# One more attention pair summed through a 128-column product, a weight difference made later, and a new block order at the start of the second product

## The chip, the cores and the metric

One core of a Trainium2 chip. The metric is device time in microseconds for one execution. Ratios are computed as the mean time of one kernel's fast runs over the mean of the other kernel's fast runs of the same rounds, so they are not quite the ratio of the medians that are quoted.

## The reference, cut to what matters

```
attention: batch 8, 8 heads, 576 positions, head size 64, window |i-j| <= 32
    attn = softmax(scale * q @ k.T inside the window);  a = attn @ v
x = a, heads side by side: 4608 x 512
h = x @ w_in (512 x 2048);  g = gelu_tanh(h);  out = g @ w_out (2048 x 512)
```

## The kernel before

The kernel walks over 9 tiles of 512 tokens. A tile first makes its hidden columns (`ffn_in`, then gelu on ScalarE), then the second product (`ffn_out`), into which the attention of the next batch is woven by a plan: at matmul number `i`, `s` makes scores, `m` multiplies by the mask, `v` makes the weighted sum, `x` normalises into `xT`. The digit is the pair (two of the eight heads, 0 to 3); 4 is the tail, the last positions of all pairs, and -1 the tail of the batch before. Tile 0 computes the second product plainly (`ffn_out_0`, 64 matmuls); later tiles use seven block products (112 matmuls) with sums of input blocks and four differences T1 to T4 of weight blocks. The differences are made once, by `combine`; T1 and T2 in tile 0, T3 and T4 in tile 1, where `i` is the number of the matmul ahead of which they are put on VectorE's queue.

```python
PLAN = {6: "s0 v-1", 24: "s1", 26: "m0", 31: "x-1", 40: "m1", 42: "v0 s2", 48: "x0", 56: "m2",
        61: "v1 s3", 64: "x1", 80: "m3", 81: "v2 s4", 88: "x2", 97: "v3", 104: "m4", 112: "x3"}
PLAN_0 = {0: "w0 w1 m0", 10: "s-1 m-1", ..., 51: "v3 c1 x3", 57: "s4 c2 m4"}    # w: cast weights, c: combine
ORDER_0 = ([(t4, 4 * w + i) for w in range(4) for t4 in (0, 1) for i in range(4)] + ...)
...
def cast_w(w, dst, on_dve=2, cs=range(4)):     # blocks 0, 1 on VectorE, 2, 3 on GpSimd
...
def weigh(b, g):                               # the weighted sum of pair g of batch b
    ...
        if fused(b, g):        # 8 products of 128 columns: V of one head beside ones
            ...
        else:                  # 16 products of 64 columns: V and ones, each for both heads
            ...
def invert(b, g, o, d):        # ScalarE: 1/sum as exp(-ln(sum)); fused: two logarithms of 64 rows
def spread(b, g, o, lt, d):    # VectorE: xT = sum * 1/sum; fused: two multiplications of 64 rows
...
todo={1: (T1, B12, B11), 2: (T2, B22, T1), 17: (T3, B22, B12), 33: (T4, B21, T2)}
```

Block product n = i // 16; product 5, so i = 80, is the first to read T4, which is B21 - T2. In the fused form one product of 128 columns gives the weighted sum of a head together with the sum by which it is divided; unfused, these are separate products of 64 columns. In VectorE's queue the changed kernel's T4 is written behind pair 1's normalisation.

The softmax here doesn't subtract the row's maximum and nothing guards it: scores larger than these inputs give would overflow.

Of the kernel before, what the change touches and what calls it, by code (L numbers as in the profile page):

```python
# [33 lines left out]
def width(pieces):  # L34
# [16 lines left out]
PLAN_0 = {0: "w0 w1 m0", 10: "s-1 m-1", 16: "s1 v-1 w2 m1 x-1", 24: "v0 s2 w3 x0", 32: "v1 m2 s3 x1",  # L51
          40: "v2 m3 x2", 48: "t4", 51: "v3 c1 x3", 57: "s4 c2 m4"}

ORDER_0 = ([(t4, 4 * w + i) for w in range(4) for t4 in (0, 1) for i in range(4)] +
           [(t4, fc) for t4 in (2, 3) for fc in range(16)])


FUSED = (3,)
# [6 lines left out]
def kernel(  # L65
# [9 lines left out]
    nc = tc.nc  # L75
# [4 lines left out]
    NF = DF // 128  # L80
# [8 lines left out]
    def load_table(which):  # L89
        nc.scalar.add_instruction(mybir.InstLoadActFuncSet(  # L90
            name=nc.get_next_instruction_name(), act_func_set_id=which, ins=[], outs=[]))
# [25 lines left out]
    Vs = [const.tile([128, 5, H + 1, 64], FP16, name=f"V{i}") for i in range(2)]  # L117
# [75 lines left out]
    def cast_w(w, dst, on_dve=2, cs=range(4)):  # L193
        for c in cs:
            (nc.vector if c < on_dve else nc.gpsimd).tensor_copy(dst[:, c, :], w[:, c, :])  # L195
# [37 lines left out]
    for i in (0, 3, 4, 1, 2):  # L233
        m, off = masks[i], 0
        for (k0, c, p0, p1) in kinds[i]:
# [6 lines left out]
                nc.vector.memset(m[k1:128, off:off + 4 * n], 0.0)  # L242
            off += 4 * n
    nc.vector.memset(ones, 1.0)
    nc.vector.memset(KTs[0][:, :, 576:640], 0.0)
    nc.vector.memset(Vs[0][64:128, 4, :, :], 0.0)

# [54 lines left out]
    def bank(i):  # L302

        return psM.tile([128, 512], FP32, name="mm", tag=f"x{i}")
# [76 lines left out]
    def fused(b, g):  # L381


        return b > 1 and g in FUSED

    def weigh(b, g, other=False):

# [68 lines left out]
    def ffn_in(t, n, d0=0, d1=4, then=True):  # L456
        fc = column(t, n)
        if n == 0 and d0 == 0:
            gTs[t] = gp.tile([128, NF, 512], FP16, name="gT", tag="gT")
        if d0 == 0:  # L460
            if t == 0 and 2 <= fc < 6:
                if fc % 2 == 0:
                    phs["S"] = psS.tile([128, 2, 512], FP32, name="ph2", tag=f"S{fc // 2 - 1}")
                phs[fc] = phs["S"][:, fc % 2, :]
            else:
                if t:
                    i = 3 if n in (1, 2) else 0 if n == 0 else (2, 1, 0)[n % 3]
                else:
                    i = fc if fc < 2 else (fc - 4) % 3
                if i == 3 and n == 1:  # L470
                    phs["S"] = psS.tile([128, 2, 512], FP32, name="ph3", tag="S0")
                phs[fc] = bank(i) if i < 2 else phs["S"][:, n - 1, :] if i == 3 else \
                    psO.tile([128, 512], FP32, name="ph", tag="D")
        ph = phs[fc]
        for dc in range(d0, d1):
            nc.tensor.matmul(ph, w_in16[:, dc, fc * 128:fc * 128 + 128],  # L476
                             xT[:, dc, t * 512 % RING:t * 512 % RING + 512],
                             start=(dc == 0), stop=(dc == 3))
        if d1 == 4 and then:
            gelu(t, n)  # L480

    def gelu(t, n):
        fc = column(t, n)
        nc.scalar.activation(gTs[t][:, fc, :], phs[fc], AF.Gelu_apprx_tanh)  # L484
        if t and n % 4 == 3:
            sums(t, n // 4)
# [3 lines left out]
    def combine_w():  # L490

        t12 = stage.tile([128, 2, 8, 256], FP16, name="t12", tag="stage")
        t34 = stage.tile([128, 2, 8, 256], FP16, name="t34", tag="stage")
        B11, B12, B21, B22 = (w_out16[:, r:r + 8, c:c + 256] for r in (0, 8) for c in (0, 256))
        T1, T2, T3, T4 = t12[:, 0], t12[:, 1], t34[:, 0], t34[:, 1]
        s12 = stage.tile([128, 2, 8, 256], FP16, name="s12", tag="stage")
        s34 = stage.tile([128, 2, 8, 256], FP16, name="s34", tag="stage")
        yo = stage.tile([128, 4, 512], FP32, name="y4", tag="stage")
        wino.update(B11=B11, B21=B21, B22=B22, T1=T1, T2=T2, T3=T3, T4=T4, S1=s12[:, 0],
                    S2=s12[:, 1], S3=s34[:, 0], S4=s34[:, 1], yo=yo,  # L500
                    todo={1: (T1, B12, B11), 2: (T2, B22, T1), 17: (T3, B22, B12),
                          33: (T4, B21, T2)})

    def combine(i):
        dst, x, y = wino["todo"][i]
        nc.vector.tensor_tensor(dst, x, y, op=ALU.subtract)  # L506
# [12 lines left out]
    pys = {}  # L519
# [3 lines left out]
    def store(t, t4, yo, cols=slice(0, 512), eng=None):  # L523
        m = 0
        while m < 128:
            b, c = divmod(t * 512 + t4 * 128 + m, S)
            q0, n = (0, cut(b)) if c < 4 * cut(b) else (cut(b), 144 - cut(b))
            j, p = divmod(c - 4 * q0, n)
            e = min(n - p, 128 - m)
            if t == NT - 1 and eng is None:  # L530
                turn_about.reverse()
            (eng or turn_about[0] if t == NT - 1 else eng or nc.gpsimd).dma_start(  # L532
                out_v[b, j, q0 + p:q0 + p + e, cols], yo[m:m + e, cols])
            m += e
# [1 line left out]
    later = []  # L536

    def ffn_out_0(t4, fc):
        if fc == 0:
            pys[t4] = bank(t4 % 2)  # L540
        nc.tensor.matmul(pys[t4], gTs[0][:, fc, t4 * 128:t4 * 128 + 128], w_out16[:, fc, :],  # L541
                         start=(fc == 0), stop=(fc == NF - 1))
        if fc == NF - 1:
            yo = yp.tile([128, 512], FP32, name="yo", tag="yo")
            nc.vector.tensor_copy(yo, pys[t4])
            if t4 == 3:
                store(0, t4, yo)
            else:
                later.append((t4, yo))
# [173 lines left out]
    for t in range(NT):  # L723
        b = t + 1
        att = b < B
        if t:
            for fc in range(begun):
                ffn_in(t, fc, 3, 4, then=False)
            for fc in range(begun):
                gelu(t, fc)  # L730
            if att and b > 1:
                cast_and_turn(b)
            for fc in range(begun, NF):
                ffn_in(t, fc)
        plan = PLAN_0 if not t else PLAN if att else {6: "v-1", 31: "x-1"} if t == B - 1 else {}

        def group(g):
            return (b, g) if g >= 0 else (b - 1, 4)

        if plan and t:  # L740
            load_table(exp_set)
        if t and b + 1 < B:
            load_qk(b + 1)
        ods = {}
        for i in range(113 if t else 65):
            for act in plan.get(i, "").split():
                kind, g = act[0], int(act[1:])
                if kind == "w":
                    cast_w(wo[g], w_out16[:, 4 * g:4 * g + 4, :])
                    if g == 2:  # L750
                        cast_v(1, 0)
                    if g == 3:
                        for pr in range(1, NPAIR):
                            cast_v(1, pr)
                        cast_vt(1)
                        cast_tails(1, nc.gpsimd)
                        load_qk(2)
                elif kind == "t":
                    pt = psS.tile([128, 2, 8, 128], FP16, name="pt", tag="S1")
                    trans_tails(1, pt[:, 0])  # L760
                elif kind == "c":
                    if g == 1:
                        combine_w()
                    combine(g)
                elif kind == "s":
                    score(*group(g))
                elif kind == "m":
                    mask(*group(g))
                elif kind == "v":
                    bb, gg = group(g)  # L770
                    o, d = weigh(bb, gg)
                    ods[g] = (o, *invert(bb, gg, o, d))
                    if t and g < 0 and b + 1 < B:
                        if t == 1:
                            nc.gpsimd.memset(Vs[1][:, :, 7, :], 1.0)
                        load_v(b + 1)
                    if t and g == (3 if att else -1):
                        load_table(gelu_set)
                else:
                    spread(*group(g), *ods[g])  # L780
            if t == 0 and i in (38, 40, 55):
                t4, yo = later.pop(0)
                store(0, t4, yo, eng=nc.scalar)
            if t == 0 and i < 64:
                ffn_out_0(*ORDER_0[i])
            elif t and i < 112:
                ffn_out(t, i)
        if t == 0:
            load_table(gelu_set)
            nc.gpsimd.memset(Vs[0][:, :, 7, :], 1.0)  # L790
            load_v(2)
        else:
            ffn_last(t)
        begun = 3 if att else 0
        for fc in range(begun):
            ffn_in(t + 1, fc, 0, 3)
# [28 lines left out]
```

## Time and profile before

| | before |
|---|---|
| median of 3 runs | 310.84 us (310.31 to 311.93) |
| span of the profiled run | 309.4 us |
| first matmul of tile 0's second product / tenth / seventeenth | 39.78 / 42.18 / 45.57 us |
| first matmul of tile 1 / of tile 2 | 60.67 / 92.89 us |
| TensorE's waits over 0.25 us from 39 us to tile 2 | 0.47 at the first, 0.36 at pair 1's sum in tile 1 |

A line of the timeline is start, duration, engine, source line, operation, out<-in, shapes and count, and in brackets the engine's idle time ahead of it and what ended it. A line of the waits view is who waited for whom, total us, times, longest. The lines themselves are in the prediction.

### The profile page before, as it was taken

What the parts mean: (1) busy time and instruction counts of PE and PEld (TensorE: products, weight loads), DVE (VectorE), ACT (ScalarE), POOL (GpSimd) and SP (SyncE); (2) the same over time, 40 slices, a digit from 0 to 9 for tenths busy, and PEclk for the clock granted to TensorE, in tenths of its full rate; (3) what the DMA queues carried; (4) which work ended last, traced back from release to release, by engine and by line L of the source; (5) the groups of instructions that cost most, each with busy time, mean ns of one, the idle gap of its engine ahead of it and who ended that gap; (6) DMA issues with size and microseconds to landing.
All of it is one profiled execution on the core that took longest, in us unless ns stands there. A gap on an engine that the chain in (4) does not pass through costs nothing.

```text
span 309.4 us, 6674 instructions
## 1 busy us (share of the span) xinstructions
PE 297.5 (96%) x2595; PEld 187.8 (61%) x2595; DVE 204.9 (66%) x461; ACT 201.9 (65%) x322; POOL 112.9 (36%) x173
## 2 busy tenths in 40 slices
PE   7889989999999999999999999999999999999993
PEld 3453545445784588448854775478647864784583
DVE  5764687787969677857786678766886654542451
ACT  1777476567677786778686877677768777606600
POOL 3658356096117420842075206720700070015000
PEclk9999999999999999999999999999999999999999
DMA  7999999999965999599859993999581031004013
GB/s 207 253 336 369 375 345 216 290 179 174 240 123 134 163 194 185 142 162 234 148 137 153 235 159 109 164 205 172 138 162 26 2 83 55 0 14 124 0 39 101
DMA packets 120254, 50.65 MB, mean 164 GB/s; under 512 B 101519, under 2 KB 113551, under 8 KB 120222
## 3 DMA queue, kind: packets, MB, share of 16 engines
q1 hardware_dynamic: 84329, 37.50, 53.6%
q0 software_dynamic: 34960, 11.54, 31.3%
q10 hardware_dynamic: 933, 1.18, 1.2%
q8 instruction: 20, 0.33, 0.4%
q14 instruction: 12, 0.10, 0.1%
HBM read 37.62 MB, written 9.44 MB: 152 GB/s over the span
## 4 chain that ended last, share of the span: by engine, by line
PE 82%; DMA 7%; SPq 5%; DVE 3%; issue 1%; POOL 1%; ACT 0%; POOLq 0%
PE mm L570 30%; PE mm L476 20%; PE ph L476 16%; PE ps_s L362 4%; PE mm L541 4%; PE ps_o L408 3%; DMA wst<-in_moe_w_out_dram 3%; DMA wst<-in_moe_w_in_dram 3%; PE ps_d L408 2%; SPq L134 2%; SPq L143 1%; POOL w_in L195 1%; SPq L186 1%; DVE t L506 1%; PE ps_o L399 1%
## 5 line engine op out<-in xcount | busy, mean ns | idle before, releaser
L476 PEld LDWEIGHTS <-w_in 128*128 128x128 f16 x576 | 56.1, 98 | 67.2 <-POOL w_in L195 1.6
L532 POOL DMA_DIRECT2D out_dram<-y x77 | 44.7, 588 | 114.8 <-DVE y L599 107.8
L476 PE MATMUL mm<-xT,w_in 128*128 128x512 f16 x320 | 78.2, 379 | 0.2 <-POOL w_in L195 0.2
L484 ACT ACTIVATE gT<-mm 128x512 f16<-128x512 f32 x80 | 47.6, 599 | 35.9 <-PE mm L476 35.2
L476 PE MATMUL ph<-xT,w_in 128*128 128x512 f16 x256 | 64.4, 379 | 0.9 <-ACT gT L484 0.7
L570 PEld LDWEIGHTS <-s 128*128 128x128 f16 x512 | 48.9, 98 | 7.0
L516 DVE TENSOR_TENSOR s<-gT 128x512 f16<-128x512 f16 x64 | 26.8, 419 | 34.4 <-ACT gT L484 34.4
L368 ACT ACTIVATE pe<-ps_s 128x704 f16<-128x704 f32 x64 | 43.3, 727 | 8.9 <-PE ps_s L362 8.0
L570 PE MATMUL mm<-t,s 128*128 128x256 f16 x376 | 45.8, 273 | 0.0
L484 ACT ACTIVATE gT<-ph 128x512 f16<-128x512 f32 x64 | 36.3, 602 | 12.3 <-PE ph L476 12.1
L570 PEld LDWEIGHTS <-gT 128*128 128x128 f16 x384 | 36.0, 98 | 7.3
L174 POOL DMA_DIRECT2D V<-in_v_dram x30 | 28.3, 964 | 23.0 <-PE ps_d L408 14.3
L426 ACT ACTIVATE lt<-ps_d 128x480 f32<-128x480 f32 (+3 forms) x34 | 18.8, 553 | 25.6 <-PE ps_d L408 25.6
L570 PE MATMUL mm<-w_out,gT 128*128 128x256 f16 x256 | 32.8, 273 | 0.0
L377 DVE TENSOR_TENSOR pe<-pe,mask 128x704 f16<-128x704 f16 x64 | 31.8, 533 | 1.1 <-ACT pe L368 1.1
L438 DVE TENSOR_TENSOR xT<-ps_o,lt 128x480 f16<-128x480 f32 (+10 forms) x38 | 20.3, 547 | 16.3 <-ACT lt L427 16.1
L427 ACT ACTIVATE lt<-lt 128x480 f32<-128x480 f32 (+3 forms) x40 | 23.5, 587 | 1.3
L90 ACT ACT_TABLE_LOAD x17 | 21.8, 1283 | 1.1 <-PEq L809 0.8
L408 PEld LDWEIGHTS <-V 128*64 128x64 f16 x288 | 15.3, 109 | 10.1 <-issue 3.6
L408 PE MATMUL ps_o<-pe,V 128*64 128x160 f16 (+2 forms) x196 | 17.5, 241 | 1.4 <-POOL V L270 1.0
L362 PE MATMUL ps_s<-QT,KT 64*128 64x192 f16 (+5 forms) x336 | 17.9, 227 | 0.7 <-DVE KT L298 0.7
L408 PE MATMUL ps_d<-pe,ones 128*64 128x160 f16 (+2 forms) x216 | 18.1, 234 | 0.0
(88 smaller groups left out, 324.2 us busy)
## 6 DMA issues: line engine op xcount, KB each, us to landing
kr<-in_k_dram SPq DMA_DIRECT2D x32, 256.0 KB, 7.2
qr<-in_q_dram SPq DMA_DIRECT2D x6, 1024.0 KB, 5.7
V<-in_v_dram POOLq DMA_DIRECT2D x30, 112.0 KB, 6.6
wst<-in_moe_w_in_dram SPq DMA_DIRECT2D x3, 1024.0 KB, 8.1
wst<-in_moe_w_out_dram SPq DMA_DIRECT2D x3, 1024.0 KB
qr<-in_q_dram SPq DMA_DIRECT2D x8, 256.0 KB
vr<-in_v_dram SPq DMA_DIRECT2D x16, 128.0 KB, 7.6
out_dram<-y POOLq DMA_DIRECT2D x24, 48.0 KB, 2.3
```

Of the source, the lines that this page charges most:

```text
L90: nc.scalar.add_instruction(mybir.InstLoadActFuncSet(name=nc.get_next_instruction_name(), act_func_set_id=which, ins=[], outs=[]))
L174: nc.gpsimd.dma_start(V[:, c, 0:7, :], v[b, 0:7, k0:k0 + 128, :].rearrange("h p d -> p h d"))
L362: nc.tensor.matmul(ps[:, h, off:off + 4 * n].rearrange("k (j p) -> k j p", j=4), KTs[b % 2][r0:r0 + 64, pr, k0:k0 + 128], QTs[b][r0:r0 + 6 ...
L368: nc.scalar.activation(pe, ps[:, :, 0:w], AF.Exp, scale=SCALE)
L377: nc.vector.tensor_tensor(pe, pe, m.rearrange("p (o w) -> p o w", o=1).broadcast_to(list(pe.shape)), op=ALU.mult)
L408: nc.tensor.matmul(bk[r0:r0 + 64, at:at + 4 * n].rearrange("d (j p) -> d j p", j=4)[:, :, p0 - q0:p1 - q0], V[:, c, 2 * pr + h + (pr == 3 ...
L427: nc.scalar.activation(lt[:, 0:n], lt[:, 0:n], AF.Exp, scale=-1.0)
L476: nc.tensor.matmul(ph, w_in16[:, dc, fc * 128:fc * 128 + 128], xT[:, dc, t * 512 % RING:t * 512 % RING + 512], start=(dc == 0), stop=(dc = ...
L484: nc.scalar.activation(gTs[t][:, fc, :], phs[fc], AF.Gelu_apprx_tanh)
L516: nc.vector.tensor_tensor(dst, x, y, op=op)
L532: (eng or turn_about[0] if t == NT - 1 else eng or nc.gpsimd).dma_start(out_v[b, j, q0 + p:q0 + p + e, cols], yo[m:m + e, cols])
L570: nc.tensor.matmul(pys["apart"][:, 0:256] if apart else py[:, blk, :], lhsT, wino[w][:, f, :], start=(new and i % (8 if one else 16) == 0) ...
```

## The change

Its intent is to take the fused form for batch 1's last pair too (fewer TensorE products), to get T4 out of the way of VectorE's busy stretch in tile 1, and to let tile 0's second product begin on the weight blocks that GpSimd has ready first.

```diff
 ORDER_0 = ([(t4, 4 * w + i) for w in range(4) for t4 in (0, 1)
-            for i in range(4)] +
+            for i in ((2, 3, 0, 1) if w == 0 else range(4))] +
@@ setup
+    nc.gpsimd.memset(Vs[1][:, :, 7, :], 1.0)
@@ fused
-        return b > 1 and g in FUSED
+        return b > 0 and g in FUSED
@@ combine_w
-                          33: (T4, B21, T2)})
+                          70: (T4, B21, T2)})
@@ ffn_out_0: the first matmul of a bank, not block 0, opens it
-        if fc == 0:
+        new = t4 not in pys
+        if new:
@@ tile 1, sum of the tail
-                        if t == 1:
-                            nc.gpsimd.memset(Vs[1][:, :, 7, :], 1.0)
```

More of the change, by code (lines that the diff above doesn't have):

```diff
@@ L52 @@
           40: "v2 m3 x2", 48: "t4", 51: "v3 c1 x3", 57: "s4 c2 m4"}
-ORDER_0 = ([(t4, 4 * w + i) for w in range(4) for t4 in (0, 1) for i in range(4)] +
+ORDER_0 = ([(t4, 4 * w + i) for w in range(4) for t4 in (0, 1)
+            for i in ((2, 3, 0, 1) if w == 0 else range(4))] +
            [(t4, fc) for t4 in (2, 3) for fc in range(16)])
@@ L538, in ffn_out_0 @@
     def ffn_out_0(t4, fc):
-        if fc == 0:
+        new = t4 not in pys
+        if new:
             pys[t4] = bank(t4 % 2)
         nc.tensor.matmul(pys[t4], gTs[0][:, fc, t4 * 128:t4 * 128 + 128], w_out16[:, fc, :],
-                         start=(fc == 0), stop=(fc == NF - 1))
+                         start=new, stop=(fc == NF - 1))
         if fc == NF - 1:
```

## The prediction

> **What bounds the kernel now.** I read the page first (busy shares, then the chain of work that ended last), then the sums over stretches for the first three steady tiles, then TensorE's waits in the two stages that the change touches, and at last the timeline of those stages. "Tile 0" and "tile 1" are the first two rounds of the kernel's second product (gelu output by output weights), with the next batch's attention woven in; i is the matmul's number in that loop.
>
> ```profile
> PE 297.5 (96%) x2595; PEld 187.8 (61%) x2595; DVE 204.9 (66%) x461; ACT 201.9 (65%) x322; POOL 112.9 (36%) x173
> ...
> PE 82%; DMA 7%; SPq 5%; DVE 3%; issue 1%; POOL 1%; ACT 0%; POOLq 0%
> ```
>
> TensorE is busy for 96% of 309.4 us and owns 82% of the chain, so only two things can shorten the kernel: fewer TensorE cycles, or one of its few idle gaps closed. The DMA and SPq shares belong to the first 41 us. Next, one tile per row, columns being stretch, length, then busy time of each engine:
>
> ```profile
> 61.30:93.50 32.20, 31.82 (x289) 20.84 (x288) 25.51 (x55) 22.80 (x39) 16.08 (x21) 1.00 1.30 179
> 93.50:125.10 31.60, 31.60 (x289) 20.86 (x288) 22.95 (x55) 23.73 (x39) 12.61 (x19) 1.00 1.19 167
> ```
>
> Tile 1 is 0.6 us longer than tile 2; tile 2 has no TensorE idle at all. Tile 1 alone makes T3 and T4, two of the four differences of weight blocks, on VectorE. All that any repair of tile 1 can win is therefore about 0.6 us, 0.2% of the time. TensorE's waits (total us, times, longest) in 36 to 62 us and then in 74 to 94 us:
>
> ```profile
> PE mm L541 <- DVE w_out L195: 0.7, 2, 0.5
> ```
> ```profile
> PE ps_o L408 <- DVE xT L438: 0.4, 1, 0.4
> ```
>
> These are the two gaps that the change aims at. The first in the timeline:
>
> ```profile
> 38.27 1.17 POOL L195 CAST w_out<-wst 128x512 f16<-128x512 f32 x2 [2.80 <-DMA wst<-in_moe_w_out_dram]
> ...
> 39.03 1.02 DVE L195 CAST w_out<-wst 128x512 f16<-128x512 f32 x2
> ...
> 39.78 2.21 PE L541 MATMUL mm<-w_out,gT 128*128 128x512 f16 x9 [0.47 <-DVE w_out L195]
> ...
> 40.95 1.18 DVE L195 CAST w_out<-wst 128x512 f16<-128x512 f32 x2 [0.90 <-DMA wst<-in_moe_w_out_dram]
> ...
> 42.18 0.38 PE L541 MATMUL mm<-w_out,gT 128*128 128x512 f16 x1 [0.19 <-DVE w_out L195]
> ```
>
> GpSimd has block 2 cast by about 38.9, but TensorE waits to 39.78 for block 0, which VectorE starts at 39.03. The reader must also see the last two rows: the second quarter of the weights lands at 40.93, VectorE casts its two blocks until 42.13, and TensorE's tenth matmul waits for the second of them, until 42.18. The second gap, in tile 1:
>
> ```profile
> 81.03 1.21 DVE L506 TENSOR_TENSOR t<-w_out,t 128x2048 f16<-128x2048 f16 x1
> ...
> 83.61 0.71 DVE L438 TENSOR_TENSOR xT<-ps_o,lt 128x384 f16<-128x384 f32 x2
> ...
> 84.37 0.26 PE L408 MATMUL ps_o<-pe,V 128*64 128x160 f16 x2 [0.36 <-DVE xT L438]
> ...
> 85.47 2.25 PE L570 MATMUL mm<-t,s 128*128 128x256 f16 x19
> ...
> 86.62 0.71 DVE L438 TENSOR_TENSOR xT<-ps_o,lt 128x384 f16<-128x384 f32 x2
> ...
> 87.55 0.27 PE L570 MATMUL mm<-t,gT 128*128 128x256 f16 x1
> ...
> 87.76 0.26 PE L408 MATMUL ps_o<-pe,V 128*64 128x160 f16 x2
> ...
> 88.46 0.34 PE L362 MATMUL ps_s<-QT,KT 64*128 64x96 f16 x8
> ...
> 90.67 0.23 PE L399 MATMUL ps_o<-pe,V 128*128 128x160 f16 x1
> ...
> 91.25 1.80 PE L570 MATMUL mm<-w_out,s 128*128 128x256 f16 x15
> ```
>
> The T4 difference (81.03) delays VectorE's queue, so that the normalised attention output (83.61) leaves its bank late and TensorE idles 0.36 us before pair 1's weighted sum (84.37). The row at 87.55 is i=80, the first matmul that reads T4. The last rows give the price of both forms of the weighted sum.
>
> **What the Trainium skill says.** "TensorE: Matmul & The Clock Gate", Part 3, The mechanism: small products placed at different column positions of the array run concurrently. The trace agrees: the two heads' 64-column products come as pairs (x2) with one start, and the 16 of them, which would need 1.1 us one after the other at the 256-column matmul's 0.109 us, take 0.70 us (87.76 to 88.46). So a 128-column form cannot halve the TensorE time. "VectorE: DVE Perf Modes", The perf-mode tier table: a 16-bit two-tensor operation on 2048 elements takes 1224 ns; the trace has 1.21. "ScalarE: Activation LUTs", What ACT_TABLE_LOAD costs: 186 ns plus 0.833 ns an element, whatever the number of rows; an estimate from that for 480 elements is 0.59 us, and the trace has 0.57 for the fused form's logarithms, though they cover 64 partitions.
>
> **The change part by part.**
>
> Fused pair. In tile 0, batch 1's last pair goes from 16 products to 8 of 128 columns. Price from tile 1: unfused 88.46 - 87.76 = 0.70 us, fused 91.25 - 90.67 = 0.58. TensorE saves 0.12 us, and from 56 us to tile 1 it has no gap, so this counts in full: -0.12. Beside it ScalarE does one more logarithm (about 0.6 us), and VectorE two multiplications of 64 rows in place of one of 128 (0.68 apiece, start to start). VectorE's queue at the end of tile 0 (T2, tail mask, last output copy, query casts) so slips by 0.5 + 0.68, some 1.15 us. Who needs it? xT of pair 3: TensorE reads it at 62.6, it will be ready at about 60.6. The accumulator bank of that copy: free at about 62.8, wanted at about 64.1. The key casts wait for their transfer until 65.08 anyway (1.54 us idle). All hidden. The ones in V move to the start on GpSimd, 0.53 us in a gap of 2.1 us before its first transfer lands: free, and so is their removal from tile 1.
>
> Order in tile 0. With blocks 2 and 3 first, TensorE starts at about 39.31 instead of 39.78, but eight matmuls of 0.215 us bring it to 41.03 and the tenth still waits for the cast that ends at 42.13, whose transfer landed at 40.93. The 0.47 us are given back as a longer wait there: 0.
>
> T4 later, first half. Without it at 81.03, VectorE runs masks, copy and normalisation about 0.7 us earlier (the copy must still wait for its matmul, 82.6), done at about 83.9. TensorE is ready at 84.01: the whole gap closes, -0.36.
>
> T4 later, second half. The change puts it at i=70, behind pair 1's normalisation in VectorE's queue. That one hangs on TensorE and ScalarE, so it keeps its place relative to TensorE: in the old times 86.62 to 87.33. T4 then runs from about 87.25 for 1.21 us, to 88.46, and with some 0.04 us of signal i=80 can start at 88.50. It would have started at 87.55. VectorE's two idle gaps, 0.86 us before 86.01 and 0.43 before 87.75, are each too short, and T4 comes after the first. TensorE stalls: +0.95. Everything later (pair 2's sum, its logarithm, normalisation, pair 3's sum) hangs on TensorE and shifts with it; pair 3's sum had 0.1 us or less of slack, so nothing is won back.
>
> Sum: -0.12 + 0 - 0.36 + 0.95 = +0.47 us, or 310.84 + 0.47 = 311.3. I take 311.2, since a smaller stall is likelier than a larger one.
>
> **The rivals.** First, T4 causes no stall, because VectorE gets to it earlier than I replayed; then the sum is -0.48 and the time 310.4. For it: VectorE catches up 0.7 us before. Against: the operation ahead of T4 waits for a logarithm and an exponential that start only after TensorE's own product, so catching up early is of no use. Second, the delayed query casts make the transposing transfers for batch 2 late. Their issue waits for VectorE (63.55 of the trace); a sibling took 6.0 us to land, so the first keys, issued at 67.55, land by about 73.5, and 1.15 us later would be 74.7, against scores at 75.1. It fits by 0.4 us; if it doesn't, up to 1 us more: 312.3. Third, the new order does win its 0.47 us, if VectorE's second pair of casts moved forward too: 310.7. Against: those wait for the transfer at 40.93, which no part of the change moves.
>
> **Range and chances.** Each part is under 1 us, and 2% is 6.2 us; no step can come near. The three runs before spread from 310.31 to 311.93, which is as wide as the effects. Range 310.2 to 312.2; within 2%: 0.98, the rest shared.
>
> **What would show it.** In the changed profile: a TensorE wait for VectorE's weight difference of about 0.9 us at i=80 in tile 1, and no wait for the normalisation at pair 1; tile 1 longer, near 32.8 us; the first product of tile 0 near 39.3 and the tenth still near 42.2; pair 3's sum in tile 0 at 0.58 us, with its two logarithms. I am wrong if i=80 does not wait, if the tenth matmul starts earlier than 42, or if the scores of tile 1's first pair wait for a transfer.

## The result, and the profile after

The changed kernel: 311.74 us median of 6 runs (310.64 to 312.19), against 310.88 (310.31 to 311.93); ratio 1.0018, 95% interval 0.9994 to 1.0043. Same within 2%, and not clear of noise. The span of the profiled run is 310.5 us.

The page of the changed kernel, busy times and then the chain of work that ended last:

```profile
PE 297.8 (96%) x2587; PEld 188.0 (61%) x2587; DVE 205.7 (66%) x462; ACT 202.5 (65%) x323; POOL 112.7 (36%) x173
...
PE 76%; DMA 9%; SPq 6%; DVE 3%; ACT 2%; POOL 1%; issue 1%; DVEq 0%; POOLq 0%
```

Eight matmuls are gone and the busy shares stand. TensorE's share of the chain is 76% instead of 82%: in this run the chain leads back from the first scores of tile 1 through the transfers of the keys. TensorE's waits from 74 to 95 us, the stretch in which before had only 0.4 us for the normalisation:

```profile
PE mm L573 <- DVE t L508: 0.8, 1, 0.8
PE ps_s L364 <- DMA KT<-k: 0.5, 1, 0.5
```

The wait for the normalisation is gone, and two others stand in its place: one for the weight difference T4, and one for the keys of batch 2. The timeline of the same stretch:

```profile
75.71 0.47 PE L364 MATMUL ps_s<-QT,KT 64*128 64x160 f16 x8 [0.47 <-DMA KT<-k]
...
84.49 0.26 PE L410 MATMUL ps_o<-pe,V 128*64 128x160 f16 x2
...
85.59 2.25 PE L573 MATMUL mm<-t,s 128*128 128x256 f16 x19
...
86.73 0.71 DVE L440 TENSOR_TENSOR xT<-ps_o,lt 128x384 f16<-128x384 f32 x2
...
87.36 1.22 DVE L508 TENSOR_TENSOR t<-w_out,t 128x2048 f16<-128x2048 f16 x1
...
88.63 0.27 PE L573 MATMUL mm<-t,gT 128*128 128x256 f16 x1 [0.79 <-DVE t L508]
```

T4 starts when pair 1's normalisation ends (87.36) and ends at 88.58; i=80 starts at 88.63. The 19 matmuls from 85.59 take 0.109 us each, so i=80 would have started at 87.66: 0.97 us lost. (The profile's idle time of 0.79 is smaller, because it counts a matmul busy until its modelled end.) The start of tile 0's second product and the fused sum at its end, from the timeline of the changed kernel:

```profile
40.37 2.40 PE L544 MATMUL mm<-w_out,gT 128*128 128x512 f16 x10
...
41.16 1.18 DVE L196 CAST w_out<-wst 128x512 f16<-128x512 f32 x2 [0.26 <-DMA wst<-in_moe_w_out_dram]
...
56.84 0.23 PE L401 MATMUL ps_o<-pe,V 128*128 128x160 f16 x1
...
57.42 0.81 PE L544 MATMUL mm<-w_out,gT 128*128 128x512 f16 x3
```

The fused sum takes 57.42 - 56.84 = 0.58 us. Where the 1.0 us of the span went, from starts in the two timelines: tenth matmul +0.22 us (42.40 against 42.18, later transfers), tile 1's first matmul -0.06, the second product of tile 1 (74.42 against 74.48) still -0.06, behind the wait for the keys +0.48, at pair 1's sum +0.12, at i=80 +1.08, tile 2's first matmul +1.08 (93.97 against 92.89), end +1.0. From tile 2 on the two kernels are the same: 216.5 us to the end in either.

### The profile page after: what moved, and what is told of

Its sections match the earlier page's. It is cut to its first block, busy times and chain, and to the rows that moved or that the text cites. A ratio compares the mean times of both kernels' runs of the same rounds, so it can differ in the third digit from the quotient of the medians.

```text
span 310.5 us, 6660 instructions
## 1 busy us (share of the span) xinstructions
PE 297.8 (96%) x2587; PEld 188.0 (61%) x2587; DVE 205.7 (66%) x462; ACT 202.5 (65%) x323; POOL 112.7 (36%) x173
## 4 chain that ended last, share of the span: by engine, by line
PE 76%; DMA 9%; SPq 6%; DVE 3%; ACT 2%; POOL 1%; issue 1%; DVEq 0%; POOLq 0%
PE mm L573 31%; PE mm L478 18%; PE ph L478 14%; PE ps_s L364 4%; DMA wst<-in_moe_w_in_dram 3%; PE ps_o L410 3%; SPq L167 3%; PE ps_d L410 2%; DMA KT<-k 2%; DMA kr<-in_k_dram 2%; DMA tr<-in_q_dram 2%; SPq L144 1%; POOL w_in L196 1%; SPq L135 1%; SPq L187 1%
## 5 line engine op out<-in xcount | busy, mean ns | idle before, releaser
L573 PE MATMUL mm<-w_out,gT 128*128 128x256 f16 x256 | 32.8, 273 | 0.0
L410 PE MATMUL ps_o<-pe,V 128*64 128x192 f16 (+3 forms) x188 | 16.7, 241 | 0.7 <-POOL V L272 0.7
```

What stands on the lines that cost most here:

```text
L410: nc.tensor.matmul(bk[r0:r0 + 64, at:at + 4 * n].rearrange("d (j p) -> d j p", j=4)[:, :, p0 - q0:p1 - q0], V[:, c, 2 * pr + h + (pr == 3 ...
L573: nc.tensor.matmul(pys["apart"][:, 0:256] if apart else py[:, blk, :], lhsT, wino[w][:, f, :], start=(new and i % (8 if one else 16) == 0) ...
```

## The experiments

The start is noisy: in fourteen profiles the second quarter of the output weights lands anywhere from 40.2 to 42.75 us, and that moves everything behind. So each run is also judged by a stretch that has none of this noise, from the start of the seventeenth matmul of tile 0's second product to the first matmul of tile 2. It holds the fused sum, the wait for the keys, pair 1's gap and the stall. All its numbers are starts in the timelines, and from tile 2 on every kernel but u_none and x_t4_all70 takes 216.5 to 216.6 us.

| run | tenth matmul starts | stretch, us | wait for keys | idle at pair 1's sum / at i=80 | timed ratio (95%) |
|---|---|---|---|---|---|
| before | 42.18 | 47.32 | 0 | 0.36 / 0 | |
| changed kernel | 42.40 | 48.24 | 0.47 | 0 / 0.79 | 1.0018 (0.9994 to 1.0043) |
| aa_before | 42.81 | 47.32 | 0 | 0.36 / 0 | 0.9999 (0.9981 to 1.0017) |
| p_fused | 43.98 | 47.15 | 0 | 0.35 / 0 | 1.0005 (0.9984 to 1.0027) |
| p_t4late | 42.65 | 47.91 | 0 | 0 / 0.80 | 1.0036 (1.0016 to 1.0055) |
| p_order | 43.70 | 47.32 | 0 | 0.36 / 0 | 1.0022 (1.0003 to 1.004) |
| x_t4_all70 | 42.42 | 47.91 | 0 | 0 / 0.80 | 1.021 (1.0193 to 1.0226) |
| x_t4_all57 | 42.04 | 46.96 | 0 | 0 / 0 | 0.9992 (0.9977 to 1.0006) |
| y_delay | 42.09 | 47.46 | 0 | 0.36 / 0 | 1.0009 (0.9996 to 1.0022) |
| z_fixq | 42.55 | 47.93 | 0.17 | 0 / 0.80 | 1.0026 (1.0009 to 1.0044) |
| z_best | 43.37 | 46.73 | 0 | 0 / 0 | 1.0007 (0.9987 to 1.0028) |
| w_two | 41.71 | 47.33 | 0.53 | 0 / 0 | 0.9982 (0.9958 to 1.0005) |
| n_nov (wrong) | 41.73 | 47.65 | 0 | 0 / 0.80 | 0.9999 (0.9978 to 1.002) |
| u_none | 43.38 | 47.37 | 0 | 0.36 / 0 | 1.0046 (1.0023 to 1.0069) |

All but n_nov gave correct results. The theory behind them: T4's slot in VectorE's queue, not its work, makes the stall; the fused sum is worth a little; the order is worth nothing; the wait for the keys comes from the slip of VectorE's queue. The rivals are named in each expectation.

**Control: the kernel before against itself (aa_before).** No edit.

> The kernel before itself, as a control of the timing: ratio 1.000. If two sets of runs of one kernel differ by 0.3 us or more, the 0.3 to 0.7 us by which the single parts lie above what their profiles add up to is scatter of the start (the landing of the second quarter of the output weights, 40.6 to 42.8 us in ten profiles). If this control lies within 0.1 us and scatters no more than the runs of before, something about the changed programs makes their start later.

Ratio 0.9999, median 311.10 us (310.56 to 311.89) against 311.15 (310.56 to 312.23). The interval is 0.18% to either side, 0.56 us, as large as the effects. The timed ratios alone cannot judge a part; the stretch can: it is 47.32 us in both profiles of this kernel, though their tenth matmuls are 0.63 us apart.

**The fused sum alone (p_fused).**

```diff
+    nc.gpsimd.memset(Vs[1][:, :, 7, :], 1.0)      # at the start, and gone from tile 1
-        return b > 1 and g in FUSED
+        return b > 0 and g in FUSED
```

> The kernel before plus the fused sum alone (batch 1's last pair from 128-column products, ones set at the start). My theory after seeing the changed kernel: TensorE spends 0.58 instead of 0.70 us on that sum in tile 0, but VectorE's queue at the end of tile 0 slips by about 1.2 to 1.5 us, the query casts with it, then the transposing transfers, so that the first scores of tile 1 wait up to 0.5 us for the first keys: net 0 to +0.4 us. Rival: the 0.47 us wait seen in the changed kernel came from a late key transfer of that one run; then no such wait here and -0.12 us.

The stretch is 0.17 us shorter, with no wait for the keys: in this profile the rival came true and my theory missed. The timed median is 310.83 us. The key wait is not a fixed companion of the fused sum.

**No fused sum at all (u_none).**

```diff
-        return b > 1 and g in FUSED
+        return False and b > 1 and g in FUSED
```

> The kernel before with no fused sum at all, so batches 2 to 7 use 16 products of 64 columns for their last pair too: the gain of the fused sum six times over, with its sign turned. By the products alone (0.70 against 0.58 us) +0.7 us; by what the changed kernel showed in tile 0 (0.17 to 0.23 us a sum) +1.0 to +1.4 us, tile 2 growing from 31.60 to about 31.8 us. Rival: the extra logarithm and multiplication of the fused form cost as much as it saves; then no change.

From tile 2's first matmul to the end it takes 217.46 us instead of 216.56, so 0.90 us for the five sums of batches 3 to 7, 0.18 us each; timed +0.46%, which is 1.4 us. That is less in all than the 1.0 to 1.4 us expected for six, and more than the 0.12 us a sum of the prediction. (Batch 2's sum, in tile 1, cost only 0.05 us: stretch 47.37. There the fused sum is entered 0.29 us behind the matmul ahead of it, and 0.13 us in most later tiles.) The gain is real and not eaten by the extra logarithm and multiplication. The timelines of before and of the changed kernel tell where the difference to 0.12 lies: three 512-column matmuls start at 56.03 in the one and at 56.19 in the other, the third of them 0.43 us later, and the next ones behind the sum start at 57.47 and 57.42. So from the third to the next is 1.01 us unfused and 0.80 fused, although the sum itself is 0.70 and 0.58: the unfused sum is also entered later (0.31 us behind that third matmul's start instead of 0.22). The starts inside the two sums tell more: from the first product to the last it is 0.55 us unfused and 0.52 fused, and from the last to the next full matmul 0.15 against 0.06. So of the 0.21 us only 0.03 lie inside; the pairs of 64-column products, whose two members start 3 to 4 ns apart, are about as fast as the 128-column products, and the rest is lost on the way in (0.09) and out (0.09).

**T4 later, alone (p_t4late).**

```diff
-                          33: (T4, B21, T2)})
+                          70: (T4, B21, T2)})
```

> The kernel before plus T4 at i=70 alone. My theory: the 0.36 us wait for the normalisation at pair 1 goes, and the first matmul that reads T4 waits 0.95 us: tile 1 grows from 32.2 to about 32.8 us, net +0.6 us. Rival: later is better, -0.36 us, no wait at i=80.

The stretch grows by 0.59 us, as worked out (-0.36 + 0.95); timed 1.0036, 95% interval 1.0016 to 1.0055. TensorE's waits in this run from 46 us on show the stall and nothing at pair 1 (the second row is the last tile's, and every kernel has it):

```profile
PE mm L570 <- DVE t L506: 0.8, 1, 0.8
PE ph L476 <- ACT gT L484: 0.7, 1, 0.7
```

**The stall multiplied (x_t4_all70), and the same work in another slot (x_t4_all57).**

```diff
-        if t == 1 and i > 2 and i in wino["todo"]:
+        if t and i > 2 and i in wino["todo"] and (t == 1 or i == 70):     # or i == 57
```

> The kernel before, with T4 made at i=70 in every tile from 1 to 8 instead of once at i=33 in tile 1 (same values each time): the disputed stall, multiplied. My theory: +0.6 us in tile 1, +0.95 us in each of tiles 2 to 6, +0.2 us in tiles 7 and 8, which have no attention ahead of it: about +5.8 us, 316.7 us. Rival (no stall, the difference fits beside TensorE): 310.5 to 311.

> As the run with T4 in every tile, but at i=57, right behind pair 2's masks, where VectorE had been idle for 0.86 us. My theory: the same eight extra differences now cost next to nothing, because the slot and not the work made the stall: 310.2 to 311.2 us, and no wait at i=80. Rival (the 1.2 us of extra VectorE work is what costs): as much as at i=70, about 316 us.

At i=70 the kernel takes 317.28 us, ratio 1.021. From tile 2 on it takes 221.73 us, 5.17 more than before, where 5 x 0.95 + 2 x 0.2 = 5.15 had been expected. At i=57 the same eight differences cost nothing: 216.54 us from tile 2 on, 310.54 us timed. Tile 2 of that run in the timeline:

```profile
116.07 1.22 DVE L506 TENSOR_TENSOR t<-w_out,t 128x2048 f16<-128x2048 f16 x1
...
117.20 0.69 DVE L590 TENSOR_TENSOR y<-mm,y 128x512 f32<-128x512 f32 x1
...
118.56 0.27 PE L570 MATMUL mm<-t,gT 128*128 128x256 f16 x1
```

T4 starts at 116.07, behind pair 2's masks, fills the time in which VectorE had waited for TensorE, and pushes the next copy only a little; i=80 starts at 118.56 without a wait. TensorE's waits of the run at i=70, from 46 to 300 us, have seven for T4 (an eighth, of 0.17 us, follows in tile 8 at 306.76):

```profile
PE mm L570 <- DVE t L506: 4.7, 7, 0.8
```

The two runs do the same VectorE work, 6.7 us apart in their medians. This shows that the slot makes the stall. In tile 1 the run at i=57 also closes the 0.36 us gap at pair 1: its stretch is 46.96.

**The new order alone (p_order).**

```diff
+            for i in ((2, 3, 0, 1) if w == 0 else range(4))] +      # and the bank opened by its first matmul
```

> The kernel before plus the new order of tile 0's first eight matmuls alone. My theory: they start up to 0.47 us earlier, and the tenth still starts when the second quarter's second cast ends, within 0.1 us of the end of that cast; 0 us net. Rival: in runs where the start of the kernel is late, as in the changed kernel's profile, the tenth does not wait and up to 0.3 us is won.

In the timeline:

```profile
40.45 0.38 PE L543 MATMUL mm<-w_out,gT 128*128 128x512 f16 x1
...
42.47 1.18 DVE L196 CAST w_out<-wst 128x512 f16<-128x512 f32 x2 [1.04 <-DMA wst<-in_moe_w_out_dram]
...
43.70 0.38 PE L543 MATMUL mm<-w_out,gT 128*128 128x512 f16 x1 [0.38 <-DVE w_out L196]
```

The first matmul starts as soon as GpSimd's first cast ends (40.40), and the tenth at 43.70, 0.05 us after the second cast of the second quarter (ends 43.65). Take the start of VectorE's first cast of that quarter as its landing. In eleven of the fourteen profiles, with the old order or the new, the tenth matmul starts 1.23 or 1.24 us behind it. The changed kernel's profile, whose first matmuls were late, is among them (cast ends 42.34, tenth 42.40). In three with the old order (x_t4_all70, x_t4_all57, w_two) the transfer came early beside the rest, and the tenth started 1.42 to 1.53 us behind it, held up by TensorE itself: there the new order could win up to 0.3 us at the tenth, as the rival has it. But the seventeenth starts 4.55 to 4.62 us behind the landing in all fourteen, in those three too. What the tenth gains is given back before the seventeenth, and the profiles show where. The seventeenth starts 0.05 to 0.09 us behind VectorE's first cast of the third quarter, and ahead of that cast stands the mask of the tail. In x_t4_all70 and w_two the mask starts 3.12 us behind the landing instead of 2.8 to 2.9, but takes 0.63 and 0.65 us instead of 0.85 to 0.99 (x_t4_all57 lies between: 3.01 and 0.74); it ends 3.74 to 3.81 us behind the landing in all fourteen. Why the mask takes longer when it starts earlier, no run tells. The stretch behind it is unchanged. The timed ratio is 1.0022, its interval just clear of 1, which the profile doesn't explain; that stays open below.

**VectorE's queue slipped on purpose (y_delay).**

```diff
-          51: "v3 c1 x3", 57: "s4 c2 m4"}
+          51: "v3 c1 x3", 57: "s4 c2 c2 c2 m4"}
```

> The kernel before with T2 made three times over in tile 0, so that VectorE's queue slips by 2.26 us before the query casts and nothing else changes. If the late query casts make the first keys of batch 2 late (they are issued behind the query transposes, about 10.6 us from the end of the query casts to the landing), the first scores of tile 1 wait 0.8 to 1.3 us and the kernel is that much longer. If the key transfer from HBM decides, there is no wait beyond 0.5 us and the time stays within 0.3 us.

The first branch of this expectation, the wait, missed; the second came, with a timed +0.28 us. The query casts came late, at 63.98 instead of 61.61 us, but the first scores did not wait for the keys:

```profile
65.98 3.51 SPq L321 DMA_TRANSPOSE QT<-q  x1
69.59 5.33 SPq L327 DMA_TRANSPOSE KT<-k  x4
```

The first keys were issued at 69.59, later than in the changed kernel (69.21), and the scores ran at 75.22: the keys took at most 5.63 us. The stretch grew by 0.14 us only. So the slip of VectorE's queue is not enough to make the wait; the time that the transfer takes has to be long as well.

**T2 moved behind the query casts (z_fixq).**

```diff
-          51: "v3 c1 x3", 57: "s4 c2 m4"}
+          51: "v3 c1 x3", 57: "s4 m4"}
@@ cast_and_turn
         queries(qr, q16, 0, 128)
+        if b == 2:
+            combine(2)
```

> The changed kernel with T2 moved from the end of tile 0 to behind the query casts of tile 1, into the idle time in which VectorE waits for the keys. My theory: the query casts come 1.1 us earlier, the first scores of tile 1 no longer wait (0.47 us won against the changed kernel), the stall at i=80 stays: about +0.5 us against the kernel before. Rival: the wait stays.

Half a miss: the query casts came at 62.14 (63.10 in the changed kernel) and the first keys were issued at 68.50 instead of 69.21, and still the scores waited 0.17 us. The keys took until about 75.57, 7.1 us. This run together with y_delay made me drop the theory that the slip alone decides, and look at the transfer.

**The competing load taken away (n_nov).** Batch 2 multiplies with batch 0's V.

```diff
             nc.gpsimd.memset(Vs[0][:, :, 7, :], 1.0)
-            load_v(2)
```

> Wrong result on purpose: the changed kernel without the load of batch 2's V, which competes with the key transposes at the start of tile 1. If that competition sets how long the keys take, the third key transfer lands in under 5.5 us instead of 5.7 to 7.5, and the first scores of tile 1 do not wait; the stall at i=80 stays. If the keys take 6 us or more even so, the wait comes from elsewhere.

The issue-to-landing row of the key transposes from 66 to 76.5 us, in the changed kernel, then in this run. It is recorded for the third of the four:

```profile
DMA to landing us min/median/max: 6.7/6.7/6.7
```
```profile
DMA to landing us min/median/max: 4.1/4.1/4.1
```

Without the load of V, which GpSimd issues in the same microseconds, the third keys land in 4.1 us; in the thirteen other profiles it was 5.4 to 7.5. There is no wait for the keys, and the stall at i=80 stays. So the competition with V's load costs the key transfers 1.3 us or more; this rests on one profile without the load, whose number lies clear of the thirteen with it.

**T4 at i=57 in the changed kernel, with T2 moved (z_best), and in the kernel before with the fused sum alone (w_two).** z_best is z_fixq with `57: (T4, B21, T2)`; w_two is p_fused with `57: (T4, B21, T2)`.

> The changed kernel with T2 behind the query casts and T4 at i=57. My theory: neither the wait for the keys nor the stall at i=80, and the gap at pair 1 closed too: -0.12 -0.36 = about -0.5 us against the kernel before, some 310.4 us; tile 1 as long as tile 2, 31.6 us. If T4 at i=57 makes pair 1's or pair 2's sum wait instead, 0.3 us of it is lost.

> The kernel before with two parts only: the fused sum, and T4 at i=57 instead of i=70. From the profiles so far: 0.2 us for the sum, 0.36 us for the gap at pair 1, no stall at i=80; from the 17th matmul of tile 0 to tile 2 it takes 46.75 us (before: 47.32), about -0.55 us in all, 310.3 us. If the first scores of tile 1 wait for the keys, up to 0.5 us of that is lost in the profiled run.

z_best has the shortest stretch, 46.73 us, 0.59 less than before, with none of the three waits; its tenth matmul was late (43.37) and its median is 311.08 us, so the expected 310.4 was not reached. w_two has a median of 310.45 us, the lowest of all, ratio 0.9982, interval 0.9958 to 1.0005: not clear of noise. In its profile the keys took 0.53 us too long:

```profile
PE ps_s L363 <- DMA KT<-k: 0.5, 1, 0.5
```

so its stretch is that of before. By the profiles a version with the fused sum, T4 at i=57 and keys in time is worth 0.55 to 0.6 us, 0.2%. The timing doesn't show it: such a gain would be a ratio of 0.9981, which lies just below z_best's interval (0.9987 to 1.0028) and inside w_two's.

**What makes the wait for the keys.** Two numbers decide it: the margin, from the issue of the first keys to the time at which TensorE would start the scores, and the time of the transfer. The scores need the first keys, but the landing is recorded for the third; in the three runs that waited the first took about 6.5, 7.1 and 7.0 us by the start of the scores, 0.2 to 0.4 less than the third. With that taken off, the table is in order: p_fused and y_delay, whose third keys took a little longer than the margin, have no wait.

| run | margin, us | third keys' transfer, us | wait |
|---|---|---|---|
| before | 7.7 | 6.0 | 0 |
| x_t4_all70 | 7.7 | 7.5 | 0 |
| x_t4_all57 | 7.6 | 7.1 | 0 |
| z_best | 7.5 | 6.0 | 0 |
| z_fixq | 6.9 | 7.3 | 0.17 |
| p_fused | 6.5 | 6.7 | 0 |
| w_two | 6.5 | 7.3 | 0.53 |
| n_nov | 6.2 | 4.1 | 0 |
| changed kernel | 6.0 | 6.7 | 0.47 |
| y_delay | 5.6 | 5.7 | 0 |

With the queue as it was, the margin is 7.5 to 8.0 us (aa_before, p_order, p_t4late and u_none, not listed, included), and no transfer seen took longer than that. The fused sum's slip (query casts at 63.10 instead of 61.61) cuts it to 6.0 to 6.5, inside the spread of the transfers, so some executions wait and others don't. How often, these single profiles can't tell.

**Left open.** Timed differences lie 0.3 to 0.8 us above what the stretches, and in x_t4_all70 and u_none the tiles behind, add up to in six runs: p_order +0.7 us for 0, p_t4late +1.1 for 0.6, x_t4_all70 +6.5 for 5.8, u_none +1.4 for 0.95, z_best +0.2 for -0.6, p_fused +0.2 for -0.2. In the changed kernel, n_nov and w_two they lie 0.3 to 0.6 below. The control's interval allows for about half a microsecond either way. A later start of these programs, by the transfers of the first 42 us, would do it too, but the profiles don't show one that goes with an edit: the second quarter lands at 41.3 us in the mean of the six kernels that set the ones of V at the start and at 41.4 in the other eight profiles, at 41.5 with the new order and 41.3 with the old. Twelve kernels of one profile each cannot separate the two.

## Why the prediction was right or wrong

Forecast: 311.2 us (310.2 to 312.2), +0.47 us from the parts; measured: 311.74, +0.18%, which is 0.56 us, with an interval of -0.2 to +1.3 us. So the timing alone could not tell the forecast from no change at all; the parts are judged by the profiles.

- **The bound.** Right: behind the tenth matmul, whose start hangs on the landing of the weights, all that was gained or lost was a wait or a product of TensorE; from tile 2 on nothing changed (216.5 us).
- **T4, both halves.** Right in mechanism and size. The gap of 0.36 us closed (stretch of x_t4_all57 46.96 against 47.32), the stall came at i=80 with 0.97 us for 0.95 forecast, the net alone is 0.59 (p_t4late) for 0.59. The rival without a stall fell with x_t4_all70.
- **The order: 0.** Right: the tenth matmul hangs on the landing and the casts of the second quarter in eleven of fourteen profiles, the seventeenth in all, and p_order's stretch is that of before. The forecast start of the first matmul near 39.3 was not seen (40.37): in that run TensorE itself was late, with the first scores at 39.97 instead of 38.85, while GpSimd had block 2 cast by 39.20.
- **The fused sum: -0.12.** Right sign, size too small. It is 0.17 in p_fused and 0.18 a sum in u_none. The mis-sized term is the price counted from the first product's start to the next matmul's: it holds the slower way out of the 64-column products (0.15 us against 0.06) and leaves out the slower way in, 0.09 us.
- **"All hidden" in the fused part.** This step failed in the profiled run. VectorE's queue slipped by 1.49 us (63.10 against 61.61), not by 1.15, the first keys were issued 1.66 us later (69.21 against 67.55), and the wait for the keys, my second rival and one of my three signs of being wrong, came: 0.47 us. With it tile 1 took 33.36 us (from 60.61 to 93.97) and not 32.8. The working of that rival took one sibling's 6.0 us as the time of a transfer; it is 5.4 to 7.5 with V's load beside it. "It fits by 0.4 us" should have read "it fits or not with the transfer of the day".
- **The sum.** Taking the measured parts, the changed kernel's stretch should be 47.32 - 0.2 + 0.6 + 0.5 = 48.2 us, and it is 48.24. That is 0.92 us more than before, twice the forecast, by the wait that was left out. That the timed mean lay near the forecast all the same is luck, as far as the record shows: executions whose keys land in time would lower the mean, but how many of the six did so is not recorded.

## What to carry to other kernels

Work moved off a busy stretch of one engine should land in a slot where that engine waits for the one that bounds the kernel, and ahead of, not behind, an operation that itself hangs on the bounding engine: here the same 1.2 us operation cost about 0.95 us a tile at i=70 and nothing at i=57. Before an engine's queue is lengthened, look up what its last operations trigger (here, transfers issued behind the casts), and set the margin against the whole spread of the transfer's time, not against one sample. When an effect is smaller than the scatter of the time, judge by a stretch between two events of the profile that the scatter doesn't reach.

## What the Trainium skill lacked or had wrong

- "TensorEngine Tiling (Array Packing)", Key Properties: it says that a change of tiling mode drains TensorE, and no page has a time for that. Here the way from full-width matmuls into pairs of 64-column products takes 0.31 us from start to start and the way out 0.15, against 0.22 and 0.06 for 128-column products; that a drain is the cause, no run shows.
- "TensorE: Matmul & The Clock Gate", Part 3, Measured speedup vs the span model: each further concurrent product is given about 4 ns. That fits inside the group, where the two products of a pair start 3 to 4 ns apart, but leaves out the way in and out, by which the unfused sum is 0.18 us dearer here.
- "DMA: Bandwidth & Descriptors", Latency and other measured facts: transposes have a rate, 261 GB/s, but no time from issue to landing, nor how it grows beside other loads. By that rate 128 x 512 two-byte elements would take 0.5 us, an estimate from the page's figure; here they took 5.4 to 7.5 us from issue to landing beside a load issued by GpSimd, and 4.1 us without it.
